# Adaptive layer norm, grouped attention and feed-forward on one core: gate columns as VectorE sums, and K groups two to four turned by the DMA crossbar

## Chip, core and metric

One core of a Trainium2 chip runs the whole block. The metric is the device time of one execution in microseconds, lower is better.

## The reference, cut to what matters

```python
mod = (_silu(c) @ w_mod).reshape(c.shape[0], 6, 1, -1)      # c: 1x1024, w_mod: 1024x6144
sa, ca, ga, sb, cb, gb = (mod[:, i] for i in range(6))      # (written out in the reference)
h = _layernorm(x) * (1 + ca) + sa                           # x: 2048 x 1024
x = x + ga * _A_ref(h, ...)      # 32 query heads, 4 K/V groups, the last 512 keys, then wo
h = _layernorm(x) * (1 + cb) + sb
x = x + gb * _B_ref(h, ...)      # silu(h @ w_gate) * (h @ w_up) @ w_down, 3584 wide
# K in attention: scores = q @ k^T, so K must stand transposed (head dimension on partitions)
```

`ga` is "the gate" here. It is needed as a row spread over all partitions, and not before the first output projection (some 265 us into the run). Each of the 6 x 8 "columns" of `mod` is 128 values, one per partition.

Of the kernel before, what the change touches and what calls it, by code (L numbers as in the profile page):

```python
# [5 lines left out]
BF16 = mybir.dt.bfloat16  # L6
F16 = mybir.dt.float16
F32 = mybir.dt.float32
P = 128
# [122 lines left out]
def bass_adaLN_cond__sliding_block_cached__swiglu_ffn__prompt_kernel(  # L132
# [14 lines left out]
    _, S, D = A_x.shape  # L147
    Hkv, Sk, Dh = A_k_cache.shape[1], A_k_cache.shape[2], A_k_cache.shape[3]
# [3 lines left out]
    W = min(4096, max(256, Sk // 4))  # L152
    rep = Hq // Hkv
    DT = D // P
    ST = S // P
    KT = W // P
# [4 lines left out]
    NJ = 6 * DT  # L161
# [11 lines left out]
    T = _Tracker()  # L173
    PE = T.stream("pe", nc.alloc_semaphore("s_pe"), nc.tensor, self_exempt=True)
    ACT = T.stream("act", nc.alloc_semaphore("s_act"), nc.scalar)
    DVE = T.stream("dve", nc.alloc_semaphore("s_dve"), nc.vector)
    POOL = T.stream("pool", nc.alloc_semaphore("s_pool"), nc.gpsimd)

    def dq(name, issuer=None):
        return T.stream(name, nc.alloc_semaphore(name), issuer or nc.sync, inc=16)  # L180

    S_ = lambda name, shape, dt: nc.alloc_sbuf_tensor(name, shape, dt)
# [3 lines left out]
    sc_bf = S_("sc_bf", [P, DT], BF16)  # L186
    mod_bf = S_("mod_bf", [P, NJ], BF16)
    c6 = S_("c6", [P, DT], F32)
    mcol = S_("mcol", [P, 3 * DT], F32)
    gain = [S_("gain%d" % i, [P, DT], BF16) for i in range(2)]  # L190
    gain_f = S_("gain_f", [P, DT], F32)
    nmean = S_("nmean", [P, 1], F32)
# [14 lines left out]
    arena = _Arena(arena_t[:, :], A_BYTES)  # L207
# [23 lines left out]
    def psap(off, dims):  # L231
        return bass.AP(tensor=ps_t, offset=off, ap=[[4096, P]] + dims)
# [29 lines left out]
    with nc.Block() as block:  # L262

        @block.gpsimd
        def _(g):
# [115 lines left out]
            def load_k(gk):  # L381
                T.op(Q_k[gk], lambda: SP.dma_start(k_nat[:, gk * KT:(gk + 1) * KT, :],
                                                   A_k_cache[0, gk, Sk - W:Sk, :].rearrange("(p k) d -> p k d", p=P)),
                     writes=[B_kn[gk]])

            def load_v(gk):
                T.op(Q_v[gk], lambda: SP.dma_start(v_aug[:, gk * KT:(gk + 1) * KT, 0:P],
                                                   A_v_cache[0, gk, Sk - W:Sk, :].rearrange("(p k) d -> p k d", p=P)),
                     writes=[B_vg[gk]])

            for hf in range(2):
# [4 lines left out]
            for k2 in range(DT // 2):  # L396
                load_wsa(k2)
            load_v(0)
            load_k(1)
            load_wq(2)  # L400
            load_x(1)
            for gk in range(2, Hkv):
                load_k(gk)
            for gk in range(1, Hkv):
                load_v(gk)
            T.op(POOL, lambda: g.memset(v_aug[:, :, P:P + 2], 1.0), writes=[B_va])  # L406

# [66 lines left out]
            def mod_mm(w_ap, wbuf, k, cols):  # L474
                for n, (j, o) in enumerate(cols):
                    mm(bank(XB, 1, 2 * o), w_ap[:, j * P:(j + 1) * P], sc_bf[:, k:k + 1],
                       k == 0 and n == 0, k == DT - 1, [wbuf, B_sc], PB[XB], skip=True)
# [94 lines left out]
            norm(2, 2, 2, 512, 512)  # L572


            B_wga = [_Buf("wga%d" % k) for k in range(DT)]
            wga = arena.at(OFF_OT[3], [DT, D], BF16, B_wga)
            GCOLS = [(j, j) for j in range(DT)]

            def load_wga(i):
                T.op(dq("q_wga%d" % i), lambda: SP.dma_start(  # L580
                    wga[:, i * HK:(i + 1) * HK, :],
                    w_mod[i * HK * P:(i + 1) * HK * P, NE * P:NE * P + D].rearrange("(k p) n -> p k n", p=P)),
                     writes=B_wga[i * HK:(i + 1) * HK])



            NF = NE + DT
            NL = NJ - NF
            B_mt = [_Buf("mt%d" % i) for i in range(2)]
            mt = [arena.at(OFF_H20 + (2 + 2 * i) * KB, [D], BF16, [B_mt[i]]) for i in range(2)]  # L590
            sc_row = arena.at(OFF_H20 + 6 * KB, [D], BF16, [B_scr])
# [2 lines left out]
            def load_mt(n):  # L594
                if n < 2:
                    for b_ in B_qT[NQT:]:
                        B_mt[n].absorb(b_)
                T.op(Q_mt[n % 2], lambda: SP.dma_start_transpose(
                    mt[n % 2].rearrange("p (a b) -> p a b", a=1), w_mod[:, (NF + n) * P:(NF + n + 1) * P]),
                     writes=[B_mt[n % 2]])  # L600

            def mod_col(n):
# [2 lines left out]
                     reads=[B_scr], writes=[B_mt[n % 2], B_mcol])  # L605

            def mod_take(g0, cbuf):
                T.op(DVE, lambda: V.tensor_copy(mod_bf[:, NF + g0 * DT:NF + (g0 + 1) * DT], mcol[:, g0 * DT:(g0 + 1) * DT]),
                     reads=[B_mcol], writes=[cbuf])


            def row_task(dst, dbuf, src, sbuf):
                T.op(ACT, lambda: A.activation(c6[:, :], src, AF.Copy), reads=[sbuf], writes=[B_c6])

                def diags(n):
                    for q in range(4):
                        col = 4 * n + q
                        T.op(ACT, lambda: A.activation(diag[q], ident, AF.Copy, scale=c6[:, col:col + 1]),  # L618
                             reads=[B_ident, B_c6], writes=[B_diag[q]])

                diags(0)
                yield
                for n in range(2):
                    for q in range(4):
                        mm(bank(XB, P, q * P), ones_bf, diag[q], q == 0, q == 3, [B_ones, B_diag[q]], PB[XB], skip=True)
                    T.op(DVE, lambda: V.tensor_copy(dst[:, n * 512:(n + 1) * 512], bank(XB)),
                         writes=[PB[XB], dbuf])
                    if n == 0:
                        diags(1)
                    yield  # L630
# [63 lines left out]
            def k_turn(gk, b):  # L694
                for kt in range(KT):
                    transpose(bank_bf(b)[:, kt * P:(kt + 1) * P], k_nat[:, gk * KT + kt, :], [B_kn[gk]], PB[b])

            def k_evac(gk, b):
                return (kT_sb[:, gk * KT:(gk + 1) * KT, :], bank_bf(b)[:, 0:KT * P].rearrange("p (a b) -> p a b", a=KT))
# [492 lines left out]
                        bgx.pop(0)  # L1192

            LOADX = {14: 2, 20: 3}
            LOADT = {14 + 4 * n: n for n in range(NL)}
            take_oT(0)
            take_oT(1)
            late = {}
# [19 lines left out]
                    next(chain[0], None)  # L1218

            def mods(i):  # L1220
                if i - 5 in LOADT:
                    n = LOADT[i - 5]
                    mod_col(n)
                    g0, last = divmod(n, DT)
                    if last == DT - 1:
                        mod_take(g0, B_late[g0 + 1])
                        if g0 == 1:
                            mod_gain(1, B_late[2], B_g[1])
                        elif g0 == 2:
                            bgx.append(row_task(rowb[1], B_row[1], mod_bf[:, 5 * DT:6 * DT], B_late[3]))  # L1230
                if i in LOADT:
                    load_mt(LOADT[i])

# [8 lines left out]
            def pre0(i):  # L1242
                if 2 <= i < NQ0:
                    q_shifted(i)
                if i in (8, 9):
                    load_wga(i - 8)
                if i in LOADX:
                    load_x(LOADX[i])
                for gk in {2: (1,), 3: (2,), 4: (3,)}.get(i, ()):
                    k_turn(gk, XB)  # L1250
                    kd, ks = k_evac(gk, XB)
                    T.op(DVE, lambda: V.tensor_copy(kd, ks), writes=[PB[XB], B_kT[gk]])
                if i == 1:
                    scores(0)
                if i in (1, 3, 5):
                    q_bias_mm(i + 1, i + 3, QB)
                if i == 1:
                    for dt in range(HK, DT):
                        shift(dt)
                if i in (8, 9):  # L1260
                    for dt in range(4 * (i - 8), 4 * (i - 8) + 4):
                        modulate(hT[1], B_hT[1], dt, 0, 0, B_mode, x1_tiles)
                if i < NQ0 + 1:
                    if i % 2 == 0:
                        qproj(NQ0 - 1 + i // 2)
                elif i + 3 < NDI:
                    qproj(i + 3)
                for n, tt in enumerate(NORMS.get(i, ())):
                    norm_turn(1, tt, x1_tiles, (i + n) % 2)
                if 1 <= i < 5:  # L1270
                    next(x1_stats[1])
                if i == 5:
                    bgx.append(row_task(sc_row, B_scr, sc_bf[:, :], B_sc))
                for k in {12: (0, 1, 2), 13: (3, 4, 5), 14: (6, 7)}.get(i, ()):
                    mod_mm(wga[:, k, :], B_wga[k], k, GCOLS)
                    if k == DT - 1:
                        T.op(DVE, lambda: V.tensor_copy(mod_bf[:, NE:NF], psap(XB * 512, [[2, DT]])), writes=[PB[XB], B_late[0]])
                        bgx.append(row_task(rowb[0], B_row[0], mod_bf[:, NE:NF], B_late[0]))
                if i == ND + 2:
                    take_oT(2)  # L1280
                    take_oT(3)
                mods(i)
                if i == 26:
                    bg.append(stats_task(2 * TPC, 2 * TPC))
# [451 lines left out]
```

## The kernel before: the parts the change touches

The first half of the attention (1024 tokens) is a chain of 64 steps, each with the query product of one head, the scores and exponentials of the head before, and the product with V of the head before that. The other work is hooked onto steps. A column of `mod` was made in one of two ways:

```python
def mod_mm(w_ap, wbuf, k, cols):           # on TensorE: 64 products of one column, 128x128 by 128x1
    for n, (j, o) in enumerate(cols):
        mm(bank(XB, 1, 2 * o), w_ap[:, j * P:(j + 1) * P], sc_bf[:, k:k + 1], ...)

def mod_col(n):                            # on VectorE: a turned weight column times the row silu(c), summed
    T.op(DVE, lambda: V.scalar_tensor_tensor(mt[n % 2], mt[n % 2], 1.0, sc_row, op0=ALU.mult,
                                             op1=ALU.mult, accum_out=mcol[:, n:n + 1]), ...)

def row_task(dst, dbuf, src, sbuf):        # 8 values a partition -> a row of 1024 on all partitions
    # ScalarE: 1 copy and 8 diagonals; TensorE: 8 products ones x diagonal; VectorE: 2 copies from PSUM
    ...

def k_turn(gk, b):                         # K group: 4 TensorE transposes into PSUM, then a copy out
    for kt in range(KT):
        transpose(bank_bf(b)[:, kt * P:(kt + 1) * P], k_nat[:, gk * KT + kt, :], [B_kn[gk]], PB[b])
```

and the steps of the first half call them like this (cut):

```python
def pre0(i):
    if i in (8, 9): load_wga(i - 8)                       # 2 x 1 MB of gate weights
    for gk in {2: (1,), 3: (2,), 4: (3,)}.get(i, ()):     # K groups two to four
        k_turn(gk, XB)
        kd, ks = k_evac(gk, XB)
        T.op(DVE, lambda: V.tensor_copy(kd, ks), ...)
    if i in (8, 9):                                       # scale and shift the second 512 tokens
        for dt in range(4 * (i - 8), 4 * (i - 8) + 4):
            modulate(hT[1], B_hT[1], dt, 0, 0, B_mode, x1_tiles)
    if i == 5:
        bgx.append(row_task(sc_row, B_scr, sc_bf[:, :], B_sc))       # the row of silu(c)
    for k in {12: (0, 1, 2), 13: (3, 4, 5), 14: (6, 7)}.get(i, ()):  # the gate's 64 products
        mod_mm(wga[:, k, :], B_wga[k], k, GCOLS)
        ...
LOADT = {14 + 4 * n: n for n in range(NL)}                # 24 columns: load at step 14+4n, sum 5 steps later
```

The softmax here doesn't subtract the row's maximum and nothing guards it: scores larger than these inputs give would overflow.

## Time and profile before

| | before |
|---|---|
| median of the first three runs | 1160.27 us (1159.91 to 1160.35) |
| span of the profiled execution | 1158.3 us |
| TensorE busy | 1148.3 us (99%) |
| VectorE / ScalarE busy | 817.4 / 532.7 us |
| column sums on VectorE | 24, each 1.22 + 0.08 us |

"Idle" in the timelines is the time an engine stood still just before a group of instructions, with what ended it. For TensorE it is counted from the modelled end of the matmul before. A matmul of 512 columns lasts 0.38 us in these records, but in a row they start 0.216 us apart, so a wait costs about 0.16 us more than its idle, and waits of less than about 0.15 us of idle are not listed. Where it matters, the text says "start to start". With TensorE busy for 99% the question for a change is only which of TensorE's instructions go and which of its few waits. Two lines of TensorE's timeline before serve as marks in everything below, a third for what comes later:

```profile
31.28 3.66 PE L272 MATMUL ps<-arena 128*128 128x512 f16 x28 [0.27 <-DVE bq L677]
...
99.79 11.14 PE L272 MATMUL ps<-arena 128*128 128x512 bf16 x98 [0.46 <-ACT arena L805]
...
499.67 151.84 PE L272 MATMUL ps<-arena 128*128 128x512 f16 x908 [0.44 <-DVE arena L835]
```

The first mark is the group of 28 matmuls behind the bias eviction. The second is the group of 98 matmuls behind step 20. Between the two lie 68.51 us; counting between marks takes out the initial loads, whose end moves from execution to execution.

### The profile page before, as it was taken

The page shows a single profiled execution, that of the slowest core. Times are in us where ns is not written, and L with a number is a line of the kernel's source. Part 1 is how long each engine was busy: PE and PEld are TensorE (multiplying, and loading weights), DVE is VectorE, ACT ScalarE, POOL GpSimd, SP SyncE. Part 2 cuts the span into 40 slices and gives each one's busy share as a digit, 9 for nine tenths or more (in the row PEclk, how much of TensorE's full clock was granted, in tenths as well). Part 3 has the DMA queues.
Part 4 walks back from the last instruction along what each step waited for, and adds up shares of the span by engine and source line. Part 5 has one row for each costly group of instructions (what it writes and reads, how often), then busy time and mean ns, then how long its engine had stood idle before and what let it go on. Part 6 is the DMA issues. An engine that isn't in the chain of part 4 may idle for free.

```text
span 1158.3 us, 18250 instructions
## 1 busy us (share of the span) xinstructions
PE 1148.3 (99%) x7105; PEld 588.0 (51%) x7105; DVE 817.4 (71%) x1638; ACT 532.7 (46%) x745; POOL 68.4 (6%) x137
## 2 busy tenths in 40 slices
PE   8999999999999999999999999999999999999999
PEld 5565556654445666656444444444444444444444
DVE  4858897757567777686567898777558777776536
ACT  3867777731127777787110354454110444544110
POOL 1100221100000111111000010000000000000000
PEclk9999999999999999999999999999999999999999
DMA  9679999976807898844875332323774424234443
GB/s 330 145 181 207 225 217 211 236 182 194 242 3 183 197 194 204 203 94 119 191 198 165 87 95 73 108 75 100 209 201 143 121 73 109 73 98 131 130 160 109
DMA packets 289941, 179.98 MB, mean 155 GB/s; under 512 B 130496, under 2 KB 278080, under 8 KB 289856
## 3 DMA queue, kind: packets, MB, share of 16 engines
q1 hardware_dynamic: 226880, 92.31, 35.5%
q10 hardware_dynamic: 54336, 55.05, 15.0%
q0 software_dynamic: 8640, 31.46, 9.3%
q8 instruction: 56, 0.92, 0.3%
q14 instruction: 29, 0.24, 0.1%
HBM read 128.45 MB, written 19.92 MB: 128 GB/s over the span
## 4 chain that ended last, share of the span: by engine, by line
PE 96%; DVE 2%; ACT 1%; DMA 1%; issue 0%; SPq 0%; ACTq 0%; DVEq 0%
PE ps L272 96%; ACT arena L805 1%; DMA arena<-in_A_wq_dram 1%; DVE arena L835 1%; DVE arena L906 0%; DVE st L413 0%; SPq L341 0%; SPq L310 0%; PE ps L276 0%; ACT arena L618 0%; DVE arena L852 0%; ACT tmp L743 0%; DVE arena L1566 0%; ACT L1551 0%; DVE arena L827 0%
## 5 line engine op out<-in xcount | busy, mean ns | idle before, releaser
L272 PE MATMUL ps<-arena 128*128 128x512 f16 (+2 forms) x6800 | 1141.2, 330 | 7.0 <-POOL arena L406 2.2
L272 PEld LDWEIGHTS ps<-arena 128*128 128x128 bf16 (+1 forms) x6800 | 577.8, 98 | 563.0 <-DVE arena L835 6.2
L805 ACT ACTIVATE arena<-ps 128x1024 bf16<-128x1024 f32 x256 | 261.5, 1022 | 44.6 <-PE ps L272 32.8
L838 ACT ACTIVATE tmp<-ps 128x512 f32<-128x512 f32 x167 | 99.7, 597 | 295.9 <-PE ps L272 280.8
L906 DVE TENSOR_TENSOR arena<-arena 128x512 f16<-128x512 bf16 x328 | 133.3, 419 | 3.0
L835 DVE TENSOR_TENSOR arena<-ps,tmp 128x512 bf16<-128x512 f32 (+1 forms) x134 | 91.8, 685 | 49.3 <-PE ps L272 37.8
L838 ACT ACTIVATE nsc<-ps 128x512 f32<-128x512 f32 x84 | 50.1, 596 | 93.2 <-PE ps L272 90.9
L827 DVE TENSOR_TENSOR arena<-ps,rl 128x512 f16<-128x512 f32 x128 | 88.5, 691 | 4.9 <-DVE rl L824 0.5
L835 DVE TENSOR_TENSOR arena<-ps,nsc 128x512 f16<-128x512 f32 x84 | 57.3, 687 | 41.2 <-PE ps L272 30.0
L824 DVE RECIPROCAL rl<-ps 128x4 f32<-128x4 f32 x128 | 23.1, 180 | 87.1 <-PE ps L272 86.2
L1551 ACT ACTIVATE arena<-arena 128x512 f16<-128x512 f16 x84 | 49.9, 624 | 32.4 <-DVE arena L835 32.4
L1122 DVE TENSOR_TENSOR tmp<-ps,tmp 128x512 f32<-128x512 f32 x32 | 22.1, 690 | 58.5 <-ACT tmp L838 48.8
L1046 DVE TENSOR_TENSOR arena<-arena 128x2048 f16<-128x2048 f16 (+3 forms) x56 | 56.0, 1010 | 9.3 <-PE ps L272 8.8
L838 ACT ACTIVATE arena<-ps 128x512 f32<-128x512 f32 x16 | 9.6, 597 | 90.5 <-PE ps L272 90.5
L956 DVE TENSOR_TENSOR arena<-arena 128x512 f16<-128x512 bf16 x120 | 47.9, 419 | 2.0 <-DMA arena<-in_A_wo_dram 0.9
L413 DVE BATCH_NORM_STATS2 st<-x_res 128x6 f32<-128x512 bf16 x58 | 39.5, 682 | 3.7 <-DMA x_res<-in_A_x_dram 3.5
L1566 DVE TENSOR_TENSOR arena<-arena 128x512 f16<-128x512 f16 x84 | 35.0, 416 | 0.3
L1123 DVE TENSOR_TENSOR tmp<-tmp,rowb 128x512 f32<-128x512 f32 (+1 forms) x49 | 33.7, 687 | 1.7
L427 DVE TENSOR_SCALAR nsc<-x_res,mv,rstd 128x1024 f16<-128x1024 bf16 (+1 forms) x30 | 16.2, 539 | 23.3 <-DMA arena<-nsc 22.4
L603 DVE SCALAR_TENSOR_TENSOR arena<-arena 128x1024 bf16<-128x1024 bf16 x24 | 29.2, 1215 | 0.0
L1124 DVE TENSOR_TENSOR arena<-tmp,x_res 128x512 bf16<-128x512 f32 (+1 forms) x33 | 22.3, 676 | 1.1
L835 DVE TENSOR_TENSOR arena<-ps,rowb 128x512 f16<-128x512 f32 x28 | 19.3, 690 | 3.9 <-ACT rowb L838 3.4
(87 smaller groups left out, 333.4 us busy)
## 6 DMA issues: line engine op xcount, KB each, us to landing
arena<-in_A_wq_dram SPq DMA_DIRECT2D x28, 512.0 KB, 5.3
arena<-wo_sum ACTq DMA_DIRECT2D x7, 2048.0 KB, 8.6
arena<-in_B_w_gate_dram SPq DMA_DIRECT2D x28, 512.0 KB, 4.0
arena<-in_B_w_up_dram SPq DMA_DIRECT2D x28, 512.0 KB, 5.1
arena<-wd_sum ACTq DMA_DIRECT2D x8, 1792.0 KB, 7.8
arena<-in_B_w_down_dram ACTq DMA_DIRECT2D x6, 1792.0 KB, 7.1
arena<-in_A_wo_dram POOLq DMA_DIRECT2D x16, 512.0 KB, 4.8
wo_sum<-arena POOLq DMA_DIRECT2D x16, 512.0 KB, 4.6
```

What stands on the lines that cost most here:

```text
L272: T.op(PE, lambda: TE.matmul(out_ap, lhsT, rhs, start=start, stop=stop, skip_group_check=skip), reads=reads, writes=[bank_buf])
L413: T.op(DVE, lambda: V.bn_stats(st_[sl][:, hf * 6:hf * 6 + 6], x_res[:, t, hf * 512:hf * 512 + 512]), reads=[B_x[t]], writes=[B_st[sl]])
L805: T.op(ACT, lambda: A.activation(ex_s[es][:, 2 * kp:2 * kp + 2, :], banks2(SCB + 2 * kp), AF.Exp, scale=att_scale), writes=[PB[SCB + 2 * k ...
L827: T.op(DVE, lambda: V.tensor_tensor(o_s[os_].rearrange("p (a b) d -> p a b d", a=2), psap(PVB * 512, [[512, 2], [130, 2], [1, P]]), rlb, A ...
L835: T.op(DVE, lambda: V.tensor_tensor(out, bank(ba), other, ADD), reads=[ob2], writes=[PB[ba], ob])
L838: T.op(ACT, lambda: A.activation(dst, bank(bk), AF.Copy), writes=[PB[bk], db])
L906: T.op(st, lambda: eng.tensor_tensor(o, a, b, op), reads=rd, writes=[wr])
L956: T.op(DVE, lambda: V.tensor_tensor(o, a, b, SUB), reads=rd, writes=[wr])
L1046: T.op(DVE, lambda: V.tensor_tensor(o, a, b, SUB), reads=rd, writes=[sb])
L1123: T.op(DVE, lambda: V.tensor_tensor(tm, tm, rw, MULT), reads=[B_row[row]], writes=[tb])
L1551: T.op(ACT, lambda: A.activation(o, s_, AF.Silu), reads=[sb], writes=[ob])
L1566: T.op(DVE, lambda: V.tensor_tensor(gu[blk][:, p, :], o, s_, MULT), reads=[sb, ob], writes=[B_gu[blk][p]])
```

## The change

It has four parts. The gate's eight columns become VectorE sums like the other 24, so there are 32, with a schedule of their own, and the gate's 64 products, its 2 MB load and its conversion go. K groups two to four are loaded already turned, by DMA transposes from DRAM, with their V in natural order to match. The row of silu(c) is built from step 8 on instead of step 5. The second tokens' modulation is split 6 + 2 instead of 4 + 4 over steps 8 and 9.

```diff
+            def load_kT(gk):
+                dst = kT_sb[:, gk * KT:(gk + 1) * KT, :].rearrange(...)
+                T.op(Q_k[gk], lambda: SP.dma_start_transpose(dst, A_k_cache[0, gk, Sk - W:Sk, :]), writes=[B_kT[gk]])
 ...   load_v: "(k p) d -> p k d" for groups two to four, "(p k) d -> p k d" for the first
-            load_k(1)
             load_wq(2)
             load_x(1)
-            for gk in range(2, Hkv):
-                load_k(gk)
             for gk in range(1, Hkv):
+                load_kT(gk)
                 load_v(gk)
 ...
-            LOADT = {14 + 4 * n: n for n in range(NL)}
+            TAKES = [12, 17, 61] + [i for i in range(15, 2 * NI - 15) if i % 4 == 3 or (i > NI + 2 and i % 4 == 2 and i % 5 in (1, 4))]
+            TAKES = sorted(TAKES)[:NL]
+            TAKET = {i: n for n, i in enumerate(TAKES)}
+            LOADT = {max(i - 4, TAKES[max(n - 2, 0)] if n > 1 else 0): n for i, n in TAKET.items()}
 ...   mods(): after the eighth sum, convert to bf16 and
+                        if g0 == 0:
+                            bgx.append(row_task(rowb[0], B_row[0], mod_bf[:, 2 * DT:3 * DT], B_late[0]))
 ...   pre0(): load_wga, k_turn / k_evac and the gate's mod_mm removed
-                    for dt in range(4 * (i - 8), 4 * (i - 8) + 4):
+                    for dt in range(6 * (i - 8), 6 if i == 8 else DT):
-                if i == 5:
+                if i == 8:
                     bgx.append(row_task(sc_row, B_scr, sc_bf[:, :], B_sc))
```

## The prediction

> **What bounds the kernel now.** I read the page's busy table first, then the chain that ended last, then TensorE's waits, then TensorE, VectorE and ScalarE in order of time over the first 200 us, where the change lives, and last the busy time by stretches.
>
> The first two parts of the page, busy time and the chain by engine:
>
> ```profile
> PE 1148.3 (99%) x7105; PEld 588.0 (51%) x7105; DVE 817.4 (71%) x1638; ACT 532.7 (46%) x745; POOL 68.4 (6%) x137
> ...
> PE 96%; DVE 2%; ACT 1%; DMA 1%; issue 0%; SPq 0%; ACTq 0%; DVEq 0%
> ```
>
> TensorE is busy for all but 10 us of 1158.3, and 96% of the chain is its own. So a gain can come only from matmuls taken away or from those 10 us. TensorE's waits:
>
> ```profile
> PE ps L272 <- POOL arena L406: 2.2, 1, 2.2
> PE ps L272 <- ACT arena L805: 1.4, 4, 0.5
> PE ps L272 <- DVE arena L835: 1.1, 3, 0.4
> PE ps L272 <- DMA arena<-in_A_wq_dram: 0.9, 1, 0.9
> PE ps L272 <- DVE arena L432: 0.5, 1, 0.5
> ```
>
> Three of them lie where the change works: part of the 1.4 us on the exponentials (L805), the 0.5 us on the modulation of the second 512 tokens (L432), and the 1.1 us on VectorE's query sums (L835). The first two in order of time, from TensorE's timeline (start, length, instructions, idle before in brackets):
>
> ```profile
> 42.06 5.23 PE L272 MATMUL ps<-arena 128*128 128x512 bf16 x50 [0.16 <-ACT arena L805]
> 47.53 0.60 PE L272 MATMUL ps<-arena 128*128 128x512 bf16 x2 [0.24 <-ACT arena L805]
> 48.65 6.09 PE L272 MATMUL ps<-arena 128*128 128x512 bf16 x54 [0.51 <-ACT arena L805]
> 55.20 2.06 PE L272 MATMUL ps<-arena 128*128 128x512 f16 x7 [0.46 <-DVE arena L432]
> ```
>
> Together 1.37 us of idle TensorE; another 0.46 us behind an exponential at 99.79 us is outside the change.
>
> **What the Trainium skill says.** "TensorE: Matmul & The Clock Gate", section "Wait — 56ns, not 53.3ns?": warm matmuls of 128 columns start 55.6 ns apart and no matmul less than about 25 ns after the last one. The trace agrees with both (below). The durations of 163 and 220 ns that the profile gives for these matmuls are latencies and must not be multiplied by the count. "VectorE: DVE Perf Modes", section "The TRN2 errata — SBUF-src ops pay a fixed extra latency per instruction", has (N+151)/0.96 ns for an fp32 sum of two tensors. With N = 1024 that is 1224 ns; the bf16 column sum here takes 1215, so it runs at one element a cycle although both operands are bf16. "DMA: Bandwidth & Descriptors", section "DMA Transpose (X-bar)", lets a DMA transpose write only to SBUF, which suits K: it lands where the scores read it, with no PSUM bank and no eviction.
>
> **The change part by part.**
>
> *The gate columns leave TensorE.* Three groups of single-column products (24, 24 and 16) go from steps 12 to 14 of the attention, where one step is one head's 512 queries. Two of those groups, with what follows each:
>
> ```profile
> 66.94 0.74 PE L272 MATMUL ps<-sc_bf,arena 128*128 128x1 bf16 x24
> 67.55 3.66 PE L272 MATMUL ps<-arena 128*128 128x512 bf16 x28
> 71.04 0.74 PE L272 MATMUL ps<-sc_bf,arena 128*128 128x1 bf16 x24
> 71.64 3.66 PE L272 MATMUL ps<-arena 128*128 128x512 bf16 x28
> ...
> 75.14 0.54 PE L272 MATMUL ps<-sc_bf,arena 128*128 128x1 bf16 x16
> 75.54 23.79 PE L272 MATMUL ps<-arena 128*128 128x512 bf16 x198
> ```
>
> Start to start: 0.61 + 0.60 + 0.40 = 1.6 us, 25 ns each. TensorE has no idle time from 55 to 99 us and the other engines have slack there, so all 1.6 us is on the path.
>
> *They come to VectorE.* Eight more column sums, each 1.22 us and 0.08 us for the accumulator, are 8 x 1.30 = 10.4 us of VectorE. By the schedule in the diff, the takes at steps 12, 15, 17 and 61 are extra in the first half of the attention, and four more (steps 74, 86, 94, 106) in the second half. In steps 12 to 17 VectorE idles about 1.7 to 1.9 us a step (for example 1.68 before the reciprocal at 69.51), so each fits. From 360 to 480 us it is busy 9.3 to 10.1 us of each 12.3 to 13.9 us stretch, so one sum in four steps fits in 3 us of slack; the added ones sit in steps without sums of the output weights. I count 0 for them.
>
> *The gate row moves.* Its eight ones-by-diagonal matmuls (8 x 56 ns) cost the same later, but its two 0.68 us copies from PSUM move from steps 16 and 17 to 40 and 44, some 165 to 178 us. There VectorE is fuller, and its query sum already held TensorE up (chain of waits, start, length):
>
> ```profile
> 123.90 0.66 DVE arena L835
> ...
> 150.67 0.66 DVE arena L835
> 151.32 0.05 issue
> 151.37 13.30 PE ps L272 x108
> ```
>
> Between 160.9 and 173.7 us VectorE is busy 11.99 of 12.8 us. The copy of step 40 falls in it, and I put the loss at 0.4 us (0 to 0.7).
>
> *Three K groups leave TensorE.* Twelve transposes, each group of four 0.22 us, make 0.66 us of TensorE, and three copies of 0.417 us, 1.25 us of VectorE. But the first group, at 30.63, stands inside a wait: TensorE waits at 31.28 for the bias eviction in any case. The other two come before the stretch in which ScalarE is never idle, and the first wait on an exponential, at 42.06, absorbs them: ScalarE's four passes for the second 512 tokens' statistics set that time and are unchanged. Worth about 0 by itself.
>
> *The row of silu(c) moves from step 5 to step 8.* I take this to matter more than K. ScalarE's timeline in the stretch that limits TensorE:
>
> ```profile
> 43.03 2.13 ACT L805 ACTIVATE arena<-ps 128x1024 bf16<-128x1024 f32 x2
> 45.06 0.20 ACT L613 ACTIVATE c<-sc_bf 128x8 f32<-128x8 bf16 x1
> 45.29 1.28 ACT L618 ACTIVATE arena<-arena,c 128x128 bf16<-128x128 bf16 x4
> 46.48 2.12 ACT L805 ACTIVATE arena<-ps 128x1024 bf16<-128x1024 f32 x2
> 48.49 1.27 ACT L618 ACTIVATE arena<-arena,c 128x128 bf16<-128x128 bf16 x4
> ```
>
> Without the 0.20 + 1.28 us at 45.06 the exponential of step 6 starts at about 45.7, when its scores are there, not 46.48. Step 7's second pair of scores then starts at 47.84 instead of 48.65: 0.8 us. With the row's matmuls gone from this place (0.5 us, paid again two steps later) and the modulation split 6 + 2 instead of 4 + 4, the wait at 55.20 shrinks from 0.46 to perhaps 0.15 us. Sum to 60 us: 0.8 + 0.5 + 0.3 - 0.5 = 1.1 us; I take 0.9, since VectorE's last two modulations may still be late.
>
> *DMA.* A direct 2 MB load goes and eight transposes of 256 KB come; three loads of 128 KB become transposes. From 34 to 54 us the queues of the traffic, nearly all of it transposes, took 54% of 16 engines for 7503 packets: 173 engine-us, 23 ns a packet. A K group is 512 packets of 256 B, so 0.74 us on 16 engines instead of about 0.37 us at the 350 GB/s of 18 to 34 us. Three cost 1.1 us more at the end of the initial loads, behind the second 512 tokens, which one small load fewer precedes. Nobody reads K's second group before step 9, near 52 us. I count 0. Natural order for V's groups two to four has the same 256 B runs: 0.
>
> Sum: -1.6 - 0.9 + 0.4 = -2.1 us, hence 1160.3 - 2.1 = 1158.2 us.
>
> **The rivals.**
>
> (1) All of it counts: 1.6 + 0.66 + the 1.37 us of waits go and nothing comes back, 1156.6 us. For it: the chain is TensorE's. Against it: ScalarE is full from 33.6 to 50 us, so work taken from TensorE there turns into waiting.
>
> (2) VectorE takes it back. In the stages 120 to 160 us it is busy 18.97 and 18.57 of 20 us; if the row copies and the added sums each delay a query sum by 0.3 to 0.6 us, ten such delays cost 3 to 5 us and the time is 1161 to 1163. Against it: apart from the row, the added sums avoid exactly that stretch, and after 165 us the only wait of TensorE in the attention is 0.44 us at 499.67.
>
> (3) The DMA queue becomes a wait. Transposes issue at 1.3 to 3.9 us each on the one queue that also turns the outputs and normalised tokens; if the second tokens' transposes land after about 49.5 us, the modulation starts late and eats the 0.9 us, and the first added gate column (loaded at step 8, used at step 12) could hold VectorE. About 1159 to 1160. Against it: that queue idles from 28.65 to 35.91 us, room for three more transposes, and a column of the mod weight lands in 5.3 us (median), against four steps of 3 to 4 us.
>
> **Range and chances.** Removed TensorE time and all reachable waits together are 3.6 us, so I can't see less than about 1155.8; a VectorE or DMA surprise of a few small stalls gives up to 1160.6. Runs of one kernel differ by 0.4 us here. Predicted 1158.2, range 1155.8 to 1160.6. Two per cent is 23 us, ten times anything above: within 2% has 0.98, the others 0.01 each.
>
> **What would show it right or wrong.** Right: 64 single-column matmuls and 12 transposes fewer on TensorE; the steps 12 to 14 shorter by 1.6 us; the waits on L805 between 42 and 49 us at most half; 32 column sums instead of 24 with no new wait of TensorE beside them; a stall of a few tenths near 165 us. Wrong: the first 60 us as long as before or longer (rival 3, seen as waits of VectorE's modulation on a DMA), or a total of waits on L835 well above 1.6 us (rival 2), or a gain over 3 us (rival 1).

## The result and the profile after

| | before | changed |
|---|---|---|
| median (same rounds, 6 runs each) | 1160.31 us (1159.84 to 1160.84) | 1158.39 us (1158.13 to 1161.15) |
| span of the profiled execution | 1158.3 us | 1156.8 us |
| TensorE busy | 1148.3 us | 1145.8 us |
| VectorE busy | 817.4 us | 825.1 us |

The ratio is 0.9988 with a 95% interval of 0.9975 to 1.0. A ratio is the mean time of one kernel's runs over that of the other's of the same rounds, so not quite the ratio of the medians; here one run of 1161.15 us pulls it up. By the 2% measure the two are the same; the medians differ by 1.92 us. The interval reaches 1.0, so these six runs alone do not settle that the change gains; a second set of the same two kernels (below, "the changed kernel again") has 0.9981, 0.9969 to 0.9994.

Line numbers moved: L805 of before is L796 of the changed kernel (exponentials), L835 is L826 (query sums), L1122 is L1113 (the first VectorE step of the output's eviction). The page's busy line and the chain by engine after:

```profile
PE 1145.8 (99%) x7029; PEld 585.5 (51%) x7029; DVE 825.1 (71%) x1651; ACT 532.0 (46%) x745; POOL 67.6 (6%) x137
...
PE 93%; DMA 2%; DVE 2%; issue 1%; ACT 1%; SPq 1%; DVEq 0%; ACTq 0%
```

76 TensorE instructions are gone (7105 - 7029), which are the 64 products and 12 transposes. TensorE's share of the chain fell and DMA's rose by one point. TensorE's waits after (in total, times, longest):

```profile
PE ps L272 <- DVE arena L826: 1.5, 5, 0.4
...
PE ps L272 <- DVE tmp L1113: 0.7, 1, 0.7
```

The wait on the modulation is gone, those on the query sums grew from 1.1 to 1.5 us, and one of 0.7 us is new. TensorE's timeline shows where:

```profile
31.43 3.66 PE L272 MATMUL ps<-arena 128*128 128x512 f16 x28 [0.51 <-DVE bq L668]
...
42.20 5.44 PE L272 MATMUL ps<-arena 128*128 128x512 bf16 x48 [0.38 <-ACT arena L796]
48.10 48.15 PE L272 MATMUL ps<-arena 128*128 128x512 bf16 x392 [0.46 <-ACT arena L796]
96.72 11.14 PE L272 MATMUL ps<-arena 128*128 128x512 bf16 x98 [0.46 <-ACT arena L796]
...
148.47 17.02 PE L272 MATMUL ps<-arena 128*128 128x512 f16 x140 [0.34 <-DVE arena L826]
165.69 100.12 PE L272 MATMUL ps<-arena 128*128 128x512 f16 x748 [0.20 <-DVE arena L826]
266.52 231.33 PE L272 MATMUL ps<-arena 128*128 128x512 f16 x1624 [0.71 <-DVE tmp L1113]
498.19 151.84 PE L272 MATMUL ps<-arena 128*128 128x512 f16 x908 [0.34 <-DVE arena L826]
```

From 48.10 us on, 392 matmuls run without a wait that the timeline lists, where before there were two more: at 48.65 after 47.53, and at 55.20. The first mark is at 31.43 us here and the second at 96.72: 65.29 us instead of 68.51, which is 3.22 us less. Then some is given back: from the second mark to the group that starts at 499.67 us before and at 498.19 us after, it is 401.47 us instead of 399.88, or 1.59 us more. After that the kernels run alike: the group at 651.90 us starts at 650.42, still 1.48 us earlier.

ScalarE's timeline, where the row of silu(c) stood between two exponentials before:

```profile
45.90 4.17 ACT L796 ACTIVATE arena<-ps 128x1024 bf16<-128x1024 f32 x4 [0.61 <-PE ps L272]
```

ScalarE now waits for TensorE at 45.90 us (0.61 us), so TensorE sets the pace there; the prediction had 45.7 us for this exponential.

The new wait at 266.52 us is the one thing nobody had expected. The chain of waits of the changed kernel leads to it (start, length, what):

```profile
252.97 9.40 DMA arena<-nsc
...
266.52 33.63 PE ps L272 x155
```

The normalised tokens of the next half stand in two buffers (`nsc`). The third normalisation must wait until the DMA transpose of the first has read its buffer. VectorE's line at that point, first in the changed kernel and then in the kernel before:

```profile
262.46 0.55 DVE L431 TENSOR_SCALAR nsc<-x_res,mv,rstd 128x1024 f16<-128x1024 bf16 x1 [4.28 <-DMA arena<-nsc]
```

```profile
259.36 0.55 DVE L427 TENSOR_SCALAR nsc<-x_res,mv,rstd 128x1024 f16<-128x1024 bf16 x1 [0.74 <-DMA arena<-nsc]
```

VectorE stood 4.28 us, and the eviction of the first output, behind it in the program, was late for TensorE. In the kernel before, VectorE stood there for 0.74 us (and 1.70 us at the fourth normalisation), and TensorE did not notice.

### The profile page after: what moved, and what is told of

Its sections match the earlier page's. It is cut to its first block, busy times and chain, and to the rows that moved or that the text cites. A ratio compares the mean times of both kernels' runs of the same rounds, so it can differ in the third digit from the quotient of the medians.

```text
span 1156.8 us, 18111 instructions
## 1 busy us (share of the span) xinstructions
PE 1145.8 (99%) x7029; PEld 585.5 (51%) x7029; DVE 825.1 (71%) x1651; ACT 532.0 (46%) x745; POOL 67.6 (6%) x137
## 4 chain that ended last, share of the span: by engine, by line
PE 93%; DMA 2%; DVE 2%; issue 1%; ACT 1%; SPq 1%; DVEq 0%; ACTq 0%
PE ps L272 93%; DMA arena<-in_A_wq_dram 1%; DMA arena<-nsc 1%; DVE arena L826 1%; ACT arena L796 1%; DMA arena<-arena 1%; DVE arena L897 0%; SPq L341 0%; DVE arena L1053 0%; DVE st L417 0%; SPq L310 0%; SPq L359 0%; DVE arena L843 0%; DVE nsc L431 0%; DVE arena L1552 0%
## 5 line engine op out<-in xcount | busy, mean ns | idle before, releaser
L796 ACT ACTIVATE arena<-ps 128x1024 bf16<-128x1024 f32 x256 | 261.2, 1021 | 43.7 <-PE ps L272 31.9
L826 DVE TENSOR_TENSOR arena<-ps,tmp 128x512 bf16<-128x512 f32 (+1 forms) x134 | 91.7, 685 | 50.7 <-PE ps L272 37.8
L826 DVE TENSOR_TENSOR arena<-ps,nsc 128x512 f16<-128x512 f32 x84 | 57.3, 686 | 41.0 <-PE ps L272 29.7
L1113 DVE TENSOR_TENSOR tmp<-ps,tmp 128x512 f32<-128x512 f32 x32 | 22.0, 689 | 61.0 <-ACT tmp L829 51.4
L594 DVE SCALAR_TENSOR_TENSOR arena<-arena 128x1024 bf16<-128x1024 bf16 x32 | 38.9, 1215 | 0.0
L826 DVE TENSOR_TENSOR arena<-ps,rowb 128x512 f16<-128x512 f32 x28 | 19.3, 689 | 3.9 <-ACT rowb L829 3.4
```

Source lines behind the costliest of these rows:

```text
L796: T.op(ACT, lambda: A.activation(ex_s[es][:, 2 * kp:2 * kp + 2, :], banks2(SCB + 2 * kp), AF.Exp, scale=att_scale), writes=[PB[SCB + 2 * k ...
L826: T.op(DVE, lambda: V.tensor_tensor(out, bank(ba), other, ADD), reads=[ob2], writes=[PB[ba], ob])
```

## The experiments

The theory going in is that of the prediction, part by part. The rivals: TensorE's instruction time is all that counts; VectorE takes it back; DMA does. Twelve runs followed, one of them the changed kernel again, all correct, each for five rounds.

### One part at a time

**The gate alone**: the change without its K part, silu row at step 5, modulation 4 + 4.

```diff
 kernel before
-  gate columns by mod_mm at steps 12 to 14, load_wga
+  TAKES / TAKET / LOADT of the change, 32 columns in mcol, gate row after the eighth
```

> Only the gate columns go to VectorE sums; K is still turned by TensorE, the row of silu(c) still at step 5, modulation still 4 + 4. Theory: the 64 single-column matmuls were on the path, so 1.6 us go by 100 us of the trace; the gate row's copy at step 40 gives back 0.3 to 0.4 us; and if the new wait of 0.7 us at the start of the output projection comes from the weight column that is now loaded at step 63, it appears here too. Time 1159.0 without that wait, 1159.7 with it, against 1160.3. Rival (TensorE's time is all that counts): 1158.7. Rival (VectorE takes it back): 1161 or more.

Measured: 1158.9 us (1158.79 to 1159.86) against 1160.26. Two lines of TensorE's timeline in this kernel:

```profile
97.36 11.14 PE L272 MATMUL ps<-arena 128*128 128x512 bf16 x98 [0.46 <-ACT arena L792]
...
149.61 17.02 PE L272 MATMUL ps<-arena 128*128 128x512 f16 x140 [0.66 <-DVE arena L822]
```

The marks are at 30.91 and 97.36 us: 66.45 us, 2.06 less than before. Of these, 0.45 us are the gate row's eight matmuls (8 x 56 ns), which now come after the second mark; 1.61 us are the products. The time alone does not separate the theory (1159.0) from the first rival (1158.7); K alone does, by its trace. The wait on VectorE near 150 us is there, and one of 0.25 us at the output projection as well. The wait of 0.66 us is longer than the 0.34 of the changed kernel; in this profile VectorE stood 0.37 us for a late load of output weights at 144.17 us, 5 us ahead of it, where the changed kernel's did not.

**K alone**:

```diff
-            load_k(1) ... load_k(gk); k_turn / k_evac at steps 2, 3, 4
+            load_kT(gk) before load_v(gk) for groups two to four, their V in natural order
```

> Only the K groups two to four are turned by the DMA crossbar, with V in natural order. Theory: the twelve transposes stood inside or ahead of waits on ScalarE, so nothing is gained: 1160.3, within 0.3 us, and TensorE's wait for the bias eviction near 31 us grows from 0.27 to about 0.5 us while the wait near 42 us grows by 0.2. Rival (TensorE's time is all that counts): 0.66 us less, 1159.6. Rival (DMA becomes a wait): above 1160.6, seen as a VectorE or TensorE wait on a DMA before 60 us.

Measured: 1160.08 us (1159.58 to 1161.07) against 1160.26.

```profile
30.85 3.66 PE L272 MATMUL ps<-arena 128*128 128x512 f16 x28 [0.51 <-DVE bq L681]
41.62 5.23 PE L272 MATMUL ps<-arena 128*128 128x512 bf16 x50 [0.38 <-ACT arena L809]
```

The second mark is at 99.35 us, so 68.50 us between the marks against 68.51. The removed transposes reappear as waits: 0.27 became 0.51 us at the bias eviction, 0.16 became 0.38 us at the exponential. The rest of their time reappears between the two, too short to be listed: the matmul at 35.40 us starts 0.44 us after the one before it, not 0.22, and the chain of waits has an exponential just ahead of it. The rival that counts TensorE's instructions falls here: 0.66 us of matmul time went and the stretch is 0.01 us shorter. DMA did not become a wait of TensorE either. ScalarE and VectorE each stood once for a load of x at 32.06 us (0.36 and 0.31 us), which neither the kernel before nor the changed one shows, and the stretch is no longer for it.

**The silu row and the modulation**:

```diff
-                if i == 5:
+                if i == 8:
                     bgx.append(row_task(sc_row, ...))
-                    for dt in range(4 * (i - 8), 4 * (i - 8) + 4):
+                    for dt in range(6 * (i - 8), 6 if i == 8 else DT):
```

> Only the silu(c) row moved from step 5 to step 8 and the modulation split 6 + 2. Theory: ScalarE's 1.48 us of row work left the stretch where it limits TensorE, so TensorE's two waits near 48 us become one of about 0.45 us and the wait on the modulation near 55 us goes: about 1.1 us, 1159.2. Rival (the transposes of K or of the second tokens set the pace): no change, 1160.3.

Measured: 1159.13 us (1158.75 to 1159.39) against 1160.26.

```profile
98.69 11.14 PE L272 MATMUL ps<-arena 128*128 128x512 bf16 x98 [0.46 <-ACT arena L805]
```

With the first mark at 31.35 us that is 67.34 us, 1.17 less than before. One wait of 0.46 us is left near 48 us, and the one near 55 us is gone.

**The silu row alone** (the first of the two edits).

> Only the silu(c) row moved from step 5 to step 8; the modulation stays 4 + 4. Theory: 0.7 us earlier at the second pair of scores of step 7, the row's eight matmuls paid later, and the wait on the modulation near 55 us remains at 0.4 us or grows, since VectorE still has four modulations left at step 9: 0.5 to 0.9 us, 1159.6. If the split is worth nothing it equals the run with both, 1159.2.

Measured: 1160.16 us (1159.77 to 1160.93) against 1160.26, so less than I had put, and within the noise.

```profile
54.40 12.35 PE L272 MATMUL ps<-arena 128*128 128x512 f16 x96 [0.46 <-DVE arena L432]
```

The second pair of scores of step 7 does start at 48.06 us, 0.7 us earlier between the marks, but the wait on the modulation stays at 0.46 us and the eight matmuls are paid later: marks at 31.39 and 99.43, 68.04 us, 0.47 less.

**The modulation split alone** (the second edit).

> The kernel before with the modulation split 6 + 2 and nothing else. Theory: the wait of 0.46 us on the modulation near 55 us goes or halves, though the silu(c) row's copy still stands ahead of it in step 8, and the waits on ScalarE near 48 us stay: 0.3 to 0.5 us less, 1159.9. If the two parts only act together: no change, 1160.3.

Measured: 1161.38 us (1159.85 to 1162.23) against 1160.55, with no gain to be seen in the time. In the profile of this kernel the initial loads ended late (the first mark is at 33.00 us, 1.7 us later than before), which the edit, of step 8, cannot have caused; whether the other runs were late for the same reason is not shown. Between the marks it is about 68.1 us, some 0.4 less; "about", because two matmul records are missing at the second mark and I took 0.23 us off for them.

```profile
56.02 12.39 PE L272 MATMUL ps<-arena 128*128 128x512 f16 x90 [0.41 <-DVE arena L656]
```

The wait on the modulation turned into one on the query copy (L656): with the silu row's copy still in step 8, six modulations ahead of that copy make it late. So the split and the move help each other: alone 0.47 and about 0.4 us, together 1.17.

The parts add up: 2.06 + 0.01 + 1.17 = 3.24 us against 3.22 in the changed kernel.

### Are the added sums hidden?

Each of the eight added sums gets a second VectorE instruction of the same length ahead of it, which leaves the data as it is (times 1, then the maximum with itself).

```diff
+                    if i in (12, 15, 17, 61, 74, 86, 94, 106):
+                        mod_twice(n)
                     mod_col(n)
```

> The changed kernel with each of the eight added column sums preceded by a second VectorE instruction of the same length that leaves the data as it is: 10.4 us more of VectorE. Theory: the added sums lie in slack; 0 to 0.5 us more, 1158.4 to 1158.9. Rival (VectorE takes the gain back through them): each costs 0.3 to 0.6 us, so 2.4 to 4.8 us more, 1161 or above.

Measured: 1159.96 us (1159.35 to 1160.77); the changed kernel has 1158.39 in its own rounds. Against the kernel before of the same rounds (1160.59) this one gains 0.63 us, the changed kernel in its rounds 1.92. The answer lies between the two: 1.3 to 1.6 us for 10.4 us of VectorE. The trace places it: the stretch between the marks (31.37 to 97.28 us) is 65.91 us, 0.62 longer than in the changed kernel. Start to start, TensorE loses 0.30 us each at 71.43 and 89.22 us, behind the doubled sums of steps 12 and 17, and nothing behind that of step 15. One wait at step 61 is new:

```profile
232.79 34.71 PE L272 MATMUL ps<-arena 128*128 128x512 f16 x206 [0.95 <-DVE arena L831]
```

In the second half of the attention, where the other four lie, no wait appeared. So the single sums were hidden, but those of steps 12, 17 and 61 have little slack left; a second sum there is too much.

### What is given back after 100 us

**The gate row later**, at steps 48 to 56, after the statistics that fill VectorE:

```diff
-                        if g0 == 0: bgx.append(row_task(rowb[0], ...))
+                if i == 45: bgx.append(row_task(rowb[0], ...))
```

> The changed kernel with the gate row built at steps 48 to 56, after the statistics of the third and fourth tokens' groups, instead of 36 to 44. Theory: the copy at step 40 cost TensorE about 0.35 us (waits of 0.34 and 0.20 us on VectorE's query sums at 148 and 166 us); later, VectorE has slack, so 0.2 to 0.4 us less than the changed kernel, 1158.1. Rival (the copy costs nothing): 1158.4.

Measured: 1158.05 us (1157.57 to 1159.04) against 1160.59 for the kernel before (ratio 0.9979, 0.9967 to 0.9992).

```profile
148.29 117.27 PE L272 MATMUL ps<-arena 128*128 128x512 f16 x888 [0.34 <-DVE arena L826]
265.83 231.33 PE L272 MATMUL ps<-arena 128*128 128x512 f16 x1624 [0.27 <-DVE tmp L1113]
```

The wait of 0.20 us at 166 us is gone; the one of 0.34 us at 148 us is not. That one isn't the row's copy. At step 35 the eighth gate sum is followed by the conversion of the eight columns (0.17 us), in a step that held TensorE up for 0.15 us already.

**One column's load two steps earlier.** My first reading of the wait at 266 us blamed the column whose DMA transpose is issued at step 63, next to three large loads.

```diff
+            LOADT[61] = LOADT.pop(63)
```

> The changed kernel with one weight column's DMA transpose issued at step 61 instead of 63. Theory: issued at 63 it lies in front of the last attention outputs' transposes and beside three large loads; they land late, VectorE starts the output sums late, the normalised tokens' transposes fall behind the 2 MB load, and TensorE waits 0.71 us at the start of the output projection. Then that wait goes here: about 0.7 us less than the changed kernel, 1157.7. Rival (that wait is DMA chance): the same as the changed kernel, 1158.4, and the wait may be there or not.

Measured: 1158.39 us (1158.17 to 1160.21), equal to the changed kernel, and the wait was 1.53 us, longer than ever. The runs fall into two groups, 1158.17 to 1158.39 and 1159.82 to 1160.21; the profiled one belongs to the second. This reading fell.

**Both edits.**

> The changed kernel with both edits, the column load at step 61 and the gate row at steps 48 to 56. Theory: the two gains add, about 1.0 us less than the changed kernel: 1157.4. If the wait at the output projection is DMA chance: 1158.1.

Measured: 1157.94 us (1157.67 to 1158.46), with a wait of 0.51 us at the output projection. The difference from the later row alone is within the noise.

With several profiles at hand, another reading offered itself. The time from the issue of the 2 MB load of output weights to the third normalisation decides:

| kernel | load to third normalisation, us | TensorE's wait, us |
|---|---|---|
| before | 5.49 | 0 |
| K alone | 9.81 | 0 |
| silu row alone | 10.14 | 0 |
| silu row and modulation | 10.33 | 0.18 |
| gate alone | 10.40 | 0.25 |
| gate row late | 10.42 | 0.27 |
| both edits | 10.66 | 0.51 |
| changed | 10.86 | 0.71 |
| load at 61 | 11.68 | 1.53 |

Whatever lies beyond some 10.15 us is TensorE's wait. Two profiles that the table leaves out fit too: the doubled sums with 10.31 us and 0.16, the modulation split alone with 9.92 and 0. The 10.15 us is the room in this program and not a time of the DMA: in the changed kernel, 4.0 us of VectorE's work lie between the start of the third normalisation and the end of the eviction that TensorE needs. In the profile of before, the first transpose of normalised tokens was issued 0.46 us before that load (253.41 and 253.87 us). In all the others it was issued after the load, by 0.7 to 4.3 us, and its buffer came free about 10 to 12 us after the load's issue. The second transpose of before was issued at 256.26 us, behind the load; its buffer came free for the fourth normalisation at 264.00, 10.13 us after the load's issue. That fits transposes that land together with the large load ahead of them, whatever their own issue time; it is a reading of profiles, and no run moved the load or the transposes to test it.

**The changed kernel again**, to try the rule on a fresh profile.

> The changed kernel once more, unaltered, on the chip of the three runs beside it. Theory: 1158.4, and in the profile a wait at the start of the output projection of anything from 0 to 1.5 us, equal to the time from the issue of the 2 MB load to the third normalisation less 10.15 us.

Measured: 1158.82 us (1158.07 to 1160.73) against 1160.55. The third normalisation came 10.77 us after the load and the wait was 0.61 us: the rule gives 0.62. The profiled execution was the slowest (1160.73), and shows another accident of the same kind, VectorE's and TensorE's line:

```profile
219.09 0.88 DVE L947 TENSOR_TENSOR arena<-arena 128x512 f16<-128x512 bf16 x2 [2.45 <-DMA arena<-in_A_wo_dram]
...
220.63 16.36 PE L272 MATMUL ps<-arena 128*128 128x512 f16 x132 [1.77 <-DVE arena L826]
```

A load of output weights landed late, VectorE stood 2.45 us in its sums, and TensorE lost 1.77 us behind it. The code of that load is in the kernel before too, where its longest stand in the profile was 0.9 us, without a wait of TensorE.

**The normalisations spaced**: two empty turns between the second and the third.

```diff
                     norm_turn(ch, tt, tiles)
                     yield
+                    if (ch, gi, tt) == (2, 0, 1):
+                        yield
+                        yield
```

> The changed kernel with two empty turns between the second and the third normalisation of the first output projection, so that VectorE never stands at the reuse of a normalisation buffer ahead of the first output's eviction. Theory: TensorE's wait of 0.2 to 1.5 us there is this stand, and its length is DMA timing; here it is absent in the profile, the median is 0.2 to 0.6 us below the changed kernel of the same rounds, and no run lies more than 0.6 us above the median. Rival (the wait only moves to a later eviction): same time as the changed kernel.

Measured: 1157.99 us (1157.2 to 1159.72), 0.8 us below the changed kernel's median of the same rounds, more than the 0.2 to 0.6 expected; the two sets of five runs overlap, so the size is not settled by the times. There is no wait at the output projection in the profile, nor in that of the next run, so it is indeed this stand that TensorE paid for, and it did not move to a later eviction. The clause on the spread failed: one run lies 1.7 us above the median, so other accidents remain.

**Spaced, gate row late, and the gate's conversion moved to step 45.**

> The changed kernel with the normalisations spaced, the gate row built at steps 48 to 56, and the gate's conversion to bf16 moved with it from step 35 to 45. Theory: the wait at the output projection goes, that of 0.20 us near 166 us goes, and that of 0.34 us near 148 us falls to the 0.15 us of the kernel before: about 0.4 us less than with the spacing alone, 1157.5. Rival (the conversion costs nothing): the 0.34 us stays, 1157.7.

Measured: 1157.46 us (1156.86 to 1157.81) against 1160.55; ratio 0.9966, 0.9954 to 0.9979. TensorE's timeline:

```profile
147.77 86.12 PE L272 MATMUL ps<-arena 128*128 128x512 f16 x697 [0.15 <-DVE arena L829]
234.20 261.88 PE L272 MATMUL ps<-arena 128*128 128x512 bf16 x1772 [0.31 <-ACT arena L799]
```

The wait near 148 us fell from 0.34 to 0.15 us, the value of the kernel before, so the conversion was its cause; the waits near 166 and 266 us are gone. This version beats both kernels, by 3.1 us and 1.4 us of the medians.

## Why the prediction was right, point by point

It named 1158.2 us; the median is 1158.39. That the two are so close is partly luck: the silu row and the modulation gave more than was put down for them, and a wait at the output projection that was not foreseen took some of it back.

- *The gate's products, -1.6 us.* Measured 1.61 us between the marks with the gate alone. The step that mattered was to take start-to-start times (25 ns) and not durations (163 ns).
- *K, 0.* Measured 0.01 us. Both places named for the absorption, the bias eviction and the first wait on an exponential, grew by 0.24 and 0.22 us; a third of the time was absorbed at 35.40 us already, behind an exponential that the prediction did not name.
- *The silu row and the modulation, -0.9 us (1.1 by the sum).* Measured 1.17 us. The size of the pair was right; how I cut it was not. For the row alone I later expected 0.5 to 0.9 us and 0.47 came. The prediction's picture of VectorE in step 8, where two modulations take the place of the row's copy, is what makes the pair worth more than its parts. One sign that the prediction named for being right did not come: the waits on the exponentials between 42 and 49 us were to fall to at most half, and went from 0.91 us (0.16, 0.24, 0.51) to 0.84 (0.38, 0.46). One wait of the three is gone, but K's transposes lengthened the first, and one of 0.46 us stays. What did come is the earlier start of the second pair of scores, 16.67 us after the first mark in the changed kernel and with the row alone, 17.37 us before, and the end of the wait on the modulation.
- *The added sums, 0.* No wait of TensorE beside them in the changed kernel. "Each fits" was true with less room than the text suggests: doubling them cost 1.3 to 1.6 us.
- *The gate row, +0.4 us.* Measured 0.20 at 166 us and 0.34 instead of 0.15 at 148 us: 0.39 us in sum. The amount was right by luck, since half of the cause was wrong: the conversion at step 35, which the prediction did not cost at all, is the other half.
- *DMA, 0.* Right for K and for the columns. (The 5.3 us given for a weight column's landing is the median over all loads of `w_mod`; for the transposed columns alone it is 4.4, so the argument had more room than it says.) But at the output projection the prediction had seen no wait to come, and in the profiled run there was one of 0.71 us. Its length varied from profile to profile as a matter of DMA timing, and it was also there (0.18 us) in a kernel without the gate sums. Whether the change makes it more frequent stays open: the profiles with gate sums and without the spacing show 0.16 to 1.53 us, the others 0 to 0.18, but each is one execution.

The balance of the two profiles, start to start: 3.22 us gained between the marks; 0.45 (the gate row's matmuls), 0.19 (the wait at 148 us) and 0.88 (output projection, listed as 0.71 of idle) given back. At 166 us a loss of 0.37 us stands where the kernel before has one of 0.19 at 164.69, too short to be listed: 0.18 more. The wait near 498 us fell by 0.09. That is 1.61 us, against 1.59 measured between the marks.

## What to carry to other kernels

When one engine is busy for 99%, work taken from it counts only where it doesn't already stand ahead of a wait: look for the next wait behind the removed instructions and ask what sets its end. Two marks in the trace, on either side of the edit, settled parts of half a microsecond that medians with a spread of one or two could not. To add up such parts, take the start of one matmul to the start of the next, not the idle that is listed. VectorE's stand at a buffer made what came after it in its program late (the spaced normalisations took TensorE's wait away), so put such a wait behind the evictions that another engine needs, not ahead of them.

## What the Trainium skill lacked or had wrong

- "TensorE: Matmul & The Clock Gate", "Part 4: PE-mode transpose", gives 275 to 390 ns for a 128x128 transpose. For a transpose it has no start-to-start time (its 55.6 ns is for other matmuls of 128 columns): here four in a row took 0.22 us, 55 ns each, with a latency of 220 ns in the record.
- "VectorE: DVE Perf Modes" has no row for a product of two tensors with a running sum in its table of modes. In bf16 with 1024 elements it took 1215 ns, plus 82 ns for a separate instruction that reads the accumulator.
- "DMA: Bandwidth & Descriptors" says, in its sections on queues, that queues share the engines, and how their packets and completions are ordered, but gives no figure for how long a large load holds back a transpose: here a transpose issued after a 2 MB load held its source buffer until 9.8 to 11.7 us after the load's issue, in eleven profiles; issued 0.46 us ahead of it, until 5.5 us, in one. An issue time of a transpose it has only in cycles and for "previous generations": here it was 1.2 to 1.3 us on the SyncE queue mostly, and in the changed kernel's profile 1.8 to 3.1 us for the three of K during the initial loads.
